# Turning attention weights by VectorE's 32x32 blocks and a DRAM scratch instead of by TensorE, in an attention and feed-forward kernel

## The chip, the cores and the metric

The kernel runs on one core of one Trainium2 chip. The metric is the device time of one execution in microseconds (us); below it is always the median of the fast runs of one kernel. Every ratio is between runs that took turns on the same chip; a difference between two experiments can go across sets of runs and chips, between which the median of the kernel before moved by 0.1%. A ratio is the mean time of one kernel's fast runs over the mean of the other's of the same rounds, so it is not quite the ratio of the medians that are quoted.

Engines: PE is TensorE's products, PEld its weight loads, DVE VectorE, ACT ScalarE, POOL GpSimd, SP SyncE, which here only issues DMAs.

## The reference, cut to what matters

```python
# q, k, v: 8 batches x 8 heads x 576 x 64, f32
scores = matmul(q, k.T) / 8
thresh = max(scores, axis=-1) - tau
attn   = exp(where(scores >= thresh, scores, -1e9) - max)   # then divided by its sum
x      = matmul(attn, v)            # (B, H, S, D) -> (B, S, 512)
xn     = (x - mean(x)) / sqrt(var(x) + 1e-6) * g_ln
out    = x + maximum(xn @ w_ch1, 0) @ w_ch2                 # 512 -> 2048 -> 512
```

All products are f32. The scores come out with queries on the partitions, and the product with v contracts over keys, so the normalised weights have to be turned in between. How they are turned is the change.

## The kernel before

A **unit** is two heads of one batch: 4 points of 128 queries for both heads, and a **rest point** (the last 64 queries of both heads together). There are 32 units, 4 per batch. A unit has 18 score products; the trace counts two records for an f32 product, so 36 records. The feed-forward part (FFN) works on groups of 512 tokens; group b is spread over the attention points of batch b + 1. A group has 128 products of 512 columns.

```python
def weights_of(u, j):                 # one point
    ...                               # TensorE: scores into sc (PSUM, two buffers)
    tensor_reduce(out=neg, in_=sc, op=max, negate=True)      # VectorE
    thr = -neg + low                                         # GpSimd
    activation(e, sc, Exp, bias=neg)                         # ScalarE
    scalar_tensor_tensor(e, sc >= thr, * e, accum_out=den)   # VectorE ("masking")
    reciprocal(den)                                          # VectorE
    e = e * den                                              # GpSimd

def turn_weights(u, j, es):
    for c in range(J):
        nc.tensor.transpose(tp[:, c], e[:, c * 128 : (c + 1) * 128], ident)
    nc.scalar.copy(em[...], tp)       # PSUM -> SBUF
    ...                               # the last 64 keys: two more transposes, two copies

def values_of(u, j):                  # after points 1, 3 and the rest point
    for c in range(J + 1):
        for h in range(2):
            nc.tensor.matmul(pv[...], lhsT=v, rhs=em)
    nc.vector.tensor_copy(x_of(g)[...], pv)
```

The program is written as one loop over points, with about two FFN steps (4 to 8 products) behind each. A scheduler then orders the instructions of each engine by its own model of their times. An engine runs its instructions in that order.

Of the kernel before, what the change touches and what calls it, by code (L numbers as in the profile page):

```python
# [8 lines left out]
F32 = mybir.dt.float32  # L9
# [9 lines left out]
def kernel(  # L19
# [44 lines left out]
    att = ctx.enter_context(tc.tile_pool(name="att", bufs=2))  # L64
    small = ctx.enter_context(tc.tile_pool(name="small", bufs=4))
    xpool = ctx.enter_context(tc.tile_pool(name="xpool", bufs=3))
    ps_sc = ctx.enter_context(tc.tile_pool(name="ps_sc", bufs=2, space=bass.MemoryType.PSUM))
# [15 lines left out]
    q_diag = [consts.tile([128, 128], F32, name=f"q_diag{i}") for i in range(2)]  # L83
    v_rest = [consts.tile([128, 2, D], F32, name=f"v_rest{i}") for i in range(3)]

# [3 lines left out]
    def load(u):  # L89


        b, hp = units[u]
        tiles = []
        for name, src in (("q", q), ("k", k)):
            t = ins.tile([128, NB, 32], F32, tag=name, name=f"{name}_in")
            for h in range(2):
                for e in range(2):
                    g = 2 * h + e
                    nc.sync.dma_start(
                        out=t[32 * g : 32 * g + 32],  # L100
                        in_=src[b, 2 * hp + h, :, 32 * e : 32 * e + 32].rearrange(
                            "(n r) c -> r n c", r=32
                        ),
                    )
            tiles.append(t)
        vt = ins.tile([128, J, 2, D], F32, tag="v", bufs=3, name="v_in")
        vr = v_rest[u % 3]
        for h in range(2):
            nc.sync.dma_start(
                out=vt[:, :, h, :],  # L110
                in_=v[b, 2 * hp + h, : J * 128, :].rearrange("(c p) d -> p c d", p=128),
            )
            nc.sync.dma_start(out=vr[64 * h : 64 * h + 64, h, :], in_=v[b, 2 * hp + h, J * 128 :, :])
        loaded[u] = (*tiles, vt, vr)
# [25 lines left out]
    )  # L140
    load(1)
    nc.gpsimd.dma_start(out=g_sb, in_=g_ln.rearrange("(c p) -> p c", p=128))
# [6 lines left out]
    def weight_steps(pool, which):  # L149
# [21 lines left out]
        for dst, src, gi in chunks:  # L171
            if src.dtype != I64:
# [4 lines left out]
                continue  # L177
            raw = pool.tile([128, WC], I64, tag="sq", name="raw")
            nc.gpsimd.dma_start(out=raw, in_=src)
            words = raw.bitcast(U32).rearrange("p (n two) -> p n two", two=2)  # L180
            lo, hi = words[:, :, 0], words[:, :, 1]
            a = pool.tile([128, WC], U32, tag="o", name="w_bits")
            r = pool.tile([128, WC], I32, tag="rb", bufs=1, name="w_low")
            m = pool.tile([128, WC], F32, tag="ot", name="w_kept")
            nc.scalar.activation(r, lo, func=AF.Copy, scale=2.0**-29)
# [17 lines left out]
            yield  # L203

    def turn(u):

        q_in, k_in = loaded[u][:2]
        qT = att.tile([128, J * 128], F32, tag="qT", name="qT")
        kT = att.tile([128, S], F32, tag="kT", name="kT")
        qd = q_diag[u % 2]  # L210
        nc.gpsimd.tensor_scalar(
            out=q_in, in0=q_in, scalar1=scl_sb, scalar2=1.0, op0=ALU.mult, op1=ALU.mult
        )
        nc.vector.transpose(kT, k_in.rearrange("p n c -> p (n c)"))  # L214
        nc.vector.transpose(qT, q_in[:, : J * 4].rearrange("p n c -> p (n c)"))
        for h in range(2):
            r = slice(64 * h, 64 * h + 64)
            nc.vector.transpose(qd[r, r], q_in[r, J * 4 :].rearrange("p n c -> p (n c)"))
        turned[u] = (qT, kT, qd)

    def weights_of(u, j):
# [20 lines left out]
        thr = small.tile([128, 2], F32, tag="thr", name="thr")  # L242
        es = []
        for i, sc in enumerate(scs):
            nc.vector.tensor_reduce(  # L245
                out=neg[:, i : i + 1], in_=sc[:, :, :HALF], axis=AXL.XY, op=ALU.max, negate=True
            )
            nc.gpsimd.tensor_scalar(  # L248
                out=thr[:, i : i + 1], in0=neg[:, i : i + 1], scalar1=-1.0, scalar2=low_sb,
                op0=ALU.mult, op1=ALU.add,  # L250
            )
            e = att.tile([128, S], F32, tag="e", bufs=4, name="e")
            nc.scalar.activation(  # L253
                e.rearrange("p (c n) -> p c n", c=2), sc[:, :, :HALF],
                func=AF.Exp, bias=neg[:, i : i + 1],
            )
            es.append(e)
        for i, (sc, e) in enumerate(zip(scs, es)):
            e2 = e.rearrange("p (c n) -> p c n", c=2)
# [12 lines left out]
    def turn_weights(u, j, es):  # L272


        if j in (0, 2, 4):
            n = 256 if j < J else 64
            em = att.tile([128, J, 2, 256], F32, tag="em", name="em")
            er = att.tile([128, 256], F32, tag="er", name="er")
            rounds[u] = (em, er, n)
        em, er, n = rounds[u]  # L280
        tr = ps_at.tile([128, 2, 128], F32, tag="at", name="tr")
        for h in range(2):
            e = es[h] if j < J else es[0]
            if j < J or h == 0:
# [3 lines left out]
                if j < J:  # L288
                    o = (j % 2) * 128
                    nc.scalar.copy(em[:, :, h, o : o + 128], tp)  # L290
                else:
                    nc.scalar.copy(
                        em[:, :, :, :64], tp.rearrange("p c (h t) -> p c h t", h=2)
                    )
# [4 lines left out]
        for h in range(2):  # L299
# [4 lines left out]
            else:  # L304
                nc.scalar.copy(er[r, :64], tr[r, h, r])  # L305

    groups = {}

# [4 lines left out]

    def values_of(u, j):

        b, hp = units[u]
        vt, vr = loaded[u][2:]
        em, er, n = rounds.pop(u)
        pv = ps_at.tile([128, 256], F32, tag="at", name="pv")
        for c in range(J + 1):  # L320
            for h in range(2):
                nc.tensor.matmul(  # L322
                    pv[64 * h : 64 * h + 64, :n],
                    lhsT=vt[:, c, h, :] if c < J else vr[:, h, :],
                    rhs=em[:, c, h, :n] if c < J else er[:, :n],
                    start=(c == 0), stop=(c == J),
                )
        t0 = b * S + (0, 0, 0, 256, 512)[j]
        at = 0
        while at < n:  # L330
            g, o = divmod(t0 + at, TOK)
            m = min(n - at, TOK - o)
            nc.vector.tensor_copy(x_of(g)[:, hp, o : o + m], pv[:, at : at + m])  # L333
            at += m
# [3 lines left out]
    def ffn_steps(g, x):  # L338

        sa = ffn.tile([128, 2, TOK], F32, tag="sq", name="sa")  # L340
        sm = ffn.tile([128, TOK], F32, tag="sm", bufs=1, name="sm")
        nc.gpsimd.tensor_tensor(out=sa, in0=x[:, 0:2], in1=x[:, 2:4], op=ALU.add)
        nc.gpsimd.tensor_tensor(out=sm, in0=sa[:, 0], in1=sa[:, 1], op=ALU.add)
        yield
        mean = ps_ff.tile([128, TOK], F32, tag="ff", name="mean")
        nc.tensor.matmul(mean, lhsT=avg_sb, rhs=sm, start=True, stop=True)
        xc = ffn.tile([128, NK, TOK], F32, tag="xc", bufs=1, name="xc")
# [4 lines left out]
        for i in range(2):  # L352
            sq = ffn.tile([128, 2, TOK], F32, tag="sq", name="sq")
            nc.scalar.activation(sq, xc[:, 2 * i : 2 * i + 2], func=AF.Square)
# [7 lines left out]
        def first(d):  # L362
            p1 = ps_ff.tile([128, TOK], F32, tag="ff", name="p1")
            for c in range(NK):
# [3 lines left out]
                )  # L368
            h = ffn.tile([128, TOK], F32, tag="h", bufs=ND + 1, name="h")
            nc.scalar.activation(h, p1, func=AF.Relu)  # L370
# [3 lines left out]
        for d in range(ND):  # L374
# [13 lines left out]
            if d == 11:  # L388
                rp = ps_ff.tile([128, TOK // 128, 128], F32, tag="ff", name="rp")
                for i in range(TOK // 128):  # L390
                    nc.tensor.transpose(
                        rp[:, i], rstd[:, i : i + 1].to_broadcast([128, 128]), ident
                    )
                rb = ffn.tile([128, TOK], F32, tag="rb", bufs=1, name="rb")
                nc.scalar.copy(rb, rp.rearrange("p i t -> p (i t)"))
                yield
        for m in range(NK):
            p2 = ps_ff.tile([128, TOK], F32, tag="ff", name="p2")
            for d in range(ND):
# [4 lines left out]
                if d % 4 == 3 and d < ND - 1:  # L404
                    yield
            o = ffn.tile([128, TOK], F32, tag="o", name="o")
            nc.vector.tensor_mul(o, p2, rb)  # L407
            nc.gpsimd.tensor_tensor(out=o, in0=o, in1=x[:, m], op=ALU.add)  # L408
            ot = ffn.tile([128, TOK // 32, 32], F32, tag="ot", name="ot")
            nc.vector.transpose(ot.rearrange("p n c -> p (n c)"), o)  # L410
            for i in range(4):
# [4 lines left out]
                    ),  # L416
                    in_=ot[32 * i : 32 * i + 32],
                )
# [35 lines left out]
    turn(0)  # L454
    held = None

    def finish(hu, hj, hes):
        turn_weights(hu, hj, hes)
        if hj in (1, 3, 4):
            values_of(hu, hj)  # L460
        if hj == J and units[hu][1] == HP - 1:
            after_batch(units[hu][0])

    for u in range(len(units)):
        for j in range(PTS):
            es = weights_of(u, j)
            if held is not None:
                finish(*held)
            held = (u, j, es)
            if j == 1 and u + 2 < len(units):  # L470
                load(u + 2)
            if j == 2 and u + 1 < len(units):
                turn(u + 1)
            for p in pumps:
                p.point()
    finish(*held)
    for p in pumps:
# [34 lines left out]
```

## Time and profile before

| part of the kernel before | us |
|---|---|
| batch 0, attention and conversion of W1 | 158 |
| batch 1, with conversion of W2 | 206 |
| batches 2 to 6 | 192 each |
| batch 7 | 188 |
| tail: the last two FFN groups | 243 |
| whole | 1757.66 (1757.14 to 1758.93, 3 runs) |

Parts are read from the starts of the FFN groups' means in the profiled run. Two rows of the page show how evenly TensorE is fed: the span in 40 slices, with its busy share in tenths and the granted TensorE clock in tenths.

```profile
PE   4889899999999999999999999999999999999998
...
PEclk9789899999999999999999999999999999999999
```

The group of the score products, with their busy time and the idle time of TensorE just before them with what ended it:

```profile
L236 PE MATMUL sc<-kT,qT 64*128 64x288 f32 x1024 | 196.0, 455 | 26.7 <-DVE kT L214 15.2 <-DVE e L260 11.5
```

Over 1024 records TensorE waited 11.5 us for VectorE's masking.

### The profile page before, as it was taken

What the parts mean: (1) busy time and instruction counts of PE and PEld (TensorE: products, weight loads), DVE (VectorE), ACT (ScalarE), POOL (GpSimd) and SP (SyncE); (2) the same over time, 40 slices, a digit from 0 to 9 for tenths busy, and PEclk for the clock granted to TensorE, in tenths of its full rate; (3) what the DMA queues carried; (4) which work ended last, traced back from release to release, by engine and by line L of the source; (5) the groups of instructions that cost most, each with busy time, mean ns of one, the idle gap of its engine ahead of it and who ended that gap; (6) DMA issues with size and microseconds to landing.
All of it is one profiled execution on the core that took longest, in us unless ns stands there. A gap on an engine that the chain in (4) does not pass through costs nothing.

```text
span 1757.6 us, 19852 instructions
## 1 busy us (share of the span) xinstructions
PE 1665.7 (95%) x6974; PEld 849.2 (48%) x6974; DVE 678.8 (39%) x1561; ACT 627.0 (36%) x1220; POOL 527.2 (30%) x789
## 2 busy tenths in 40 slices
PE   4889899999999999999999999999999999999998
PEld 2545445545554555545544555455454555444443
DVE  5766544433444334343334434444344434200000
ACT  6775863234323342234323432234223422220110
POOL 6765842232224122232233212322233122300100
PEclk9789899999999999999999999999999999999999
DMA  7423410111111111111111111101111000001001
GB/s 155 108 69 66 133 41 16 33 27 21 21 33 33 21 21 17 31 19 21 26 28 33 21 21 33 33 11 21 27 23 27 7 1 12 13 0 18 6 5 20
DMA packets 271380, 55.83 MB, mean 32 GB/s; under 512 B 267184, under 2 KB 267184, under 8 KB 271280
## 3 DMA queue, kind: packets, MB, share of 16 engines
q1 hardware_dynamic: 266640, 37.78, 12.3%
q0 software_dynamic: 4640, 16.78, 3.3%
q8 instruction: 55, 0.90, 0.2%
q14 instruction: 45, 0.37, 0.1%
HBM read 45.09 MB, written 9.44 MB: 31 GB/s over the span
## 4 chain that ended last, share of the span: by engine, by line
PE 82%; DVE 5%; ACT 5%; POOL 3%; DMA 2%; issue 2%; SPq 0%; ACTq 0%; POOLq 0%; DVEq 0%
PE p L400 27%; PE p L365 26%; PE pv L322 11%; PE sc L236 11%; PE tp L287 6%; DVE neg L245 2%; ACT e L253 2%; DMA raw<-in_moe_w_ch_dram 2%; ACT em L290 1%; DVE xc L348 1%; PE tr L296 1%; ACT er L303 1%; PE tr L298 1%; DVE e L260 1%; POOL o L408 1%
## 5 line engine op out<-in xcount | busy, mean ns | idle before, releaser
L365 PE MATMUL p<-xc,w 128*128 128x512 f32 x1152 | 541.5, 608 | 10.3 <-DVE xc L348 9.8
L400 PE MATMUL p<-h,w 128*128 128x512 f32 x1152 | 525.2, 597 | 0.0
L245 DVE TENSOR_REDUCE neg<-sc 128x1 f32<-128x576 f32 x288 | 207.3, 750 | 477.3 <-PE sc L236 476.9
L253 ACT ACTIVATE e<-sc,neg 128x576 f32<-128x576 f32 x288 | 212.5, 745 | 373.5 <-DVE neg L245 368.0
L365 PEld LDWEIGHTS p<-xc,w 128*128 128x128 f32 x1152 | 207.3, 193 | 222.1 <-issue 208.2
L400 PEld LDWEIGHTS p<-h,w 128*128 128x128 f32 x1152 | 206.6, 190 | 218.5 <-issue 218.0
L265 POOL TENSOR_SCALAR e<-e,den 128x576 f32<-128x576 f32 x288 | 215.9, 752 | 250.1 <-DVE den L264 216.9
L248 POOL TENSOR_SCALAR thr<-neg,low_sb 128x1 f32<-128x1 f32 x288 | 78.8, 274 | 625.6 <-DVE neg L245 599.0
L260 DVE SCALAR_TENSOR_TENSOR e<-sc,thr,e 128x576 f32<-128x576 f32 x288 | 232.1, 812 | 54.9 <-ACT e L253 36.4
L236 PE MATMUL sc<-kT,qT 64*128 64x288 f32 x1024 | 196.0, 455 | 26.7 <-DVE kT L214 15.2
L370 ACT ACTIVATE h<-p 128x512 f32<-128x512 f32 x144 | 85.9, 596 | 364.7 <-PE p L365 364.3
L290 ACT COPY em<-tp 128x512 f32<-128x512 f32 x256 | 149.2, 583 | 177.4 <-PE tp L287 174.9
L287 PEld LDWEIGHTS tp<-ident,e 128*128 128x128 f32 x1152 | 134.8, 145 | 145.4 <-ACT em L290 75.1
L287 PE MATMUL tp<-ident,e 128*128 128x128 f32 x1152 | 188.9, 288 | 16.8 <-ACT em L290 14.1
L322 PE MATMUL pv<-em,v_in 128*64 128x256 f32 (+1 forms) x1536 | 176.1, 350 | 7.9 <-ACT er L303 6.3
L236 PEld LDWEIGHTS sc<-kT,qT 64*128 64x128 f32 x1024 | 106.1, 198 | 136.5 <-issue 80.7
L322 PEld LDWEIGHTS pv<-em,v_in 128*64 128x64 f32 x1536 | 98.9, 142 | 114.9 <-issue 30.8
L408 POOL TENSOR_TENSOR o<-o,x 128x512 f32<-128x512 f32 x36 | 45.5, 1265 | 274.7 <-DVE o L407 274.7
L407 DVE TENSOR_TENSOR o<-p,rb 128x512 f32<-128x512 f32 x36 | 24.9, 692 | 200.7 <-PE p L400 200.7
L333 DVE COPY x<-pv 128x256 f32<-128x256 f32 (+3 forms) x120 | 35.4, 311 | 168.6 <-PE pv L322 168.6
L322 PE MATMUL pv<-er,v_rest 128*64 128x256 f32 (+1 forms) x384 | 62.9, 342 | 15.2 <-ACT er L305 15.2
L303 ACT COPY er<-tr 64x128 f32<-64x128 f32 x256 | 65.7, 257 | 2.3 <-PE tr L298 0.7
(61 smaller groups left out, 857.8 us busy)
## 6 DMA issues: line engine op xcount, KB each, us to landing
raw<-in_moe_w_ch_dram POOLq DMA_DIRECT2D x32, 512.0 KB, 4.2
q_in<-in_q_dram SPq DMA_DIRECT2D x128, 72.0 KB, 2.5
k_in<-in_k_dram SPq DMA_DIRECT2D x128, 72.0 KB, 2.3
out_dram<-ot SPq DMA_DIRECT2D x144, 64.0 KB, 1.9
v_in<-in_v_dram SPq DMA_DIRECT2D x64, 128.0 KB, 2.4
v_rest<-in_v_dram SPq DMA_DIRECT2D x64, 16.0 KB, 2.1
tau_sb<-in_tau_dram SPq DMA_DIRECT2D x1, 0.5 KB, 2.6
g_sb<-in_moe_g_ln_dram POOLq DMA_DIRECT2D x1, 2.0 KB, 3.5
```

What stands on the lines that cost most here:

```text
L236: nc.tensor.matmul(sc[:, c, :HALF], lhsT=lhsT, rhs=kT[rows, c * HALF : (c + 1) * HALF], start=True, stop=True,)
L245: nc.vector.tensor_reduce(out=neg[:, i : i + 1], in_=sc[:, :, :HALF], axis=AXL.XY, op=ALU.max, negate=True)
L253: nc.scalar.activation(e.rearrange("p (c n) -> p c n", c=2), sc[:, :, :HALF], func=AF.Exp, bias=neg[:, i : i + 1],)
L260: nc.vector.scalar_tensor_tensor(out=e2, in0=sc[:, :, :HALF], scalar=thr[:, i : i + 1], in1=e2, op0=ALU.is_ge, op1=ALU.mult, accum_out=den ...
L265: nc.gpsimd.tensor_scalar(out=e, in0=e, scalar1=den[:, i : i + 1], scalar2=1.0, op0=ALU.mult, op1=ALU.mult)
L287: nc.tensor.transpose(tp[:, c], e[:, c * 128 : (c + 1) * 128], ident)
L290: nc.scalar.copy(em[:, :, h, o : o + 128], tp)
L303: nc.scalar.copy(er[r, o : o + 128], tr[r, h])
L322: nc.tensor.matmul(pv[64 * h : 64 * h + 64, :n], lhsT=vt[:, c, h, :] if c < J else vr[:, h, :], rhs=em[:, c, h, :n] if c < J else er[:, :n ...
L365: nc.tensor.matmul(p1, lhsT=w1_sb[c][:, d * 128 : (d + 1) * 128], rhs=xc[:, c, :], start=(c == 0), stop=(c == NK - 1),)
L370: nc.scalar.activation(h, p1, func=AF.Relu)
L400: nc.tensor.matmul(p2, lhsT=w2_sb[d][:, m * 128 : (m + 1) * 128], rhs=hs[d], start=(d == 0), stop=(d == ND - 1),)
```

## The change

TensorE is the bound, and 1.25 us of each point are transposes on it. The change takes them off it from batch 1 on: VectorE turns each weight tile within 32x32 blocks, SyncE writes the blocks to a DRAM scratch so that a row of the scratch is one key, and reads it back with keys on the partitions. The value products come some points later, and their sums are copied out of PSUM by ScalarE instead of VectorE.

```diff
+    def turn_blocks(u, j, es):
+        ...
+        for h, et in enumerate(rounds[u]):
+            nc.vector.transpose(et[:, :, j % 2], es[:, h].rearrange("p (n c) -> p n c", c=32))
+            if j % 2 == 1:
+                for a in range(4):
+                    nc.sync.dma_start(out=scr[h, :, :, a]..., in_=et[32 * a : 32 * a + 32]...)
+    def fetch(j, scr):
+        ...
+        for h in range(2):
+            nc.sync.dma_start(out=em[:, h, :, :n], in_=rows[h, : J * 128]...)
+            nc.sync.dma_start(out=er[64 * h : 64 * h + 64, :n], in_=rows[h, J * 128 :])
...
-            nc.vector.tensor_copy(x_of(g)[:, hp, o : o + m], pv[:, at : at + m])
+            (nc.scalar.copy if by_blocks(u) else nc.vector.tensor_copy)(
+                x_of(g)[:, hp, o : o + m], pv[:, at : at + m]
+            )
...
+        if by_blocks(u):              # every batch but the first
+            scr = turn_blocks(u, j, es)
+            if ends:                  # points 1, 3 and the rest point
+                later(1, lambda: later(2, values, u, j, fetch(j, scr)))
```

The cuts (`...`) leave out tile shapes, the smaller buffers of q, k and the FFN that make room, and the order of the columns of q. The weights' two exponential buffers of a point (e) are one tile now, with two in all.

## The prediction

> **What bounds the kernel now.** I read the page first (busy shares), then busy time by stretch, then the chain of work that ended last in one stretch, then groups by shape, then VectorE's timeline in a stretch without feed-forward work. A line with x8 counts records; one f32 product is two records, so x8 is four products.
>
> Busy time by stretch (us; columns PE, PEld, DVE, ACT, POOL busy with counts, granted clock, DMA share, GB/s):
>
> ```profile
> core 0: us, PE busy (x) PEld busy (x) DVE busy (x) ACT busy (x) POOL busy (x), PEclk, DMA share, GB/s
> 120.00:158.00 38.00, 34.23 (x212) 21.45 (x212) 24.67 (x62) 20.10 (x44) 18.64 (x29) 0.96 0.16 28
> 158.00:365.00 207.00, 194.51 (x826) 98.14 (x828) 94.89 (x208) 100.10 (x186) 95.26 (x125) 0.96 0.25 58
> 942.00:1134.00 192.00, 187.92 (x842) 96.73 (x841) 78.20 (x187) 66.77 (x135) 51.41 (x85) 0.99 0.14 25
> 1518.00:1758.00 240.00, 227.90 (x538) 101.39 (x538) 14.57 (x21) 25.87 (x41) 20.89 (x14) 0.97 0.06 10
> ```
>
> The mean of a feed-forward (FFN) group comes at 158, 364, 556, 750, ... us. So the kernel is: batch 0, attention alone with the weight conversion, 158 us; batch 1, 207 us; batches 2 to 7, 192 us each; a tail of 240 us with only FFN. In a 192 us batch TensorE is busy 98% and VectorE 41%: TensorE is the bound. The chain in one such stretch (start, length, what) shows which TensorE work is on the path:
>
> ```profile
> 708.05 1.17 PE sc L236 x8
> 709.22 0.59 PE tp L287 x4
> 709.80 0.11 PE tr L296
> 709.91 0.11 PE tr L298
> 710.02 1.72 PE p L400 x4
> 711.74 0.44 PE tp L287 x4
> 712.18 5.15 PE p L400 x12
> ```
>
> One attention point (one 128-query block of two heads) costs 1.17 us of scores, 0.59 + 0.11 + 0.11 + 0.44 = 1.25 us of transposes, and FFN products at 5.15 / 12 x 2 = 0.86 us each fill the rest. The transposes stand on the path with nothing beside them.
>
> **What the Trainium skill says.** (1) "TensorE: Matmul & The Clock Gate", Part 2, step LDWEIGHTS: "The MATMULs themselves stay in program order"; only weight loads are pulled ahead. The trace agrees: the order of products in the timeline is that of the built program (8 score records, 4, 1, 1 transposes, 4, 4, 12). So a product that waits holds all behind it, ready or not. (2) "VectorE: DVE Perf Modes", The three transpose paths: VectorE transposes only within 32x32 blocks, so the rest has to be done by addresses, here through DRAM. In this trace a 128x576 block transpose takes 0.77 us. (3) "DMA: Bandwidth & Descriptors", Two DMAs through the same engine are not ordered: a read of what a DMA wrote has to wait at the issuing engine for the write's semaphore. So SyncE's queue stands still for it; this trace has no such pair. (4) The first page, HAM oscillation: gaps above about 3.4 us lower the clock. The trace agrees in kind: 0.78 granted in 40 to 80 us, where TensorE waits often, 0.99 in full batches.
>
> **The change part by part.**
> Removed from TensorE: per unit (two heads, 5 points; 28 units in batches 1 to 7) 36 + 10 transposes at 0.11 us (0.44 / 4) plus about 0.15 us after each score block (0.59 - 0.44): 46 x 0.11 + 5 x 0.15 = 5.8 us, x 28 = 162 us. Removed from ScalarE: the copies out of PSUM, about 7.5 us per unit.
>
> Added to VectorE: nine block transposes per unit, 9 x 0.77 = 6.9 us; the x copies (35.4 us / 32 = 1.1) go to ScalarE. VectorE's attention work per unit is then, from these rows,
>
> ```profile
> L260 DVE SCALAR_TENSOR_TENSOR e<-sc,thr,e 128x576 f32<-128x576 f32 x288 | 232.1, 812 | 54.9 <-ACT e L253 36.4 <-POOL thr L248 9.4 <-ACT em L290 0.6
> ...
> L245 DVE TENSOR_REDUCE neg<-sc 128x1 f32<-128x576 f32 x288 | 207.3, 750 | 477.3 <-PE sc L236 476.9
> ...
> L264 DVE RECIPROCAL den<-den 128x1 f32<-128x1 f32 x288 | 45.0, 161 | 5.9
> ...
> L214 DVE STREAM_TRANSPOSE kT<-k_in 128x576 f32<-128x576 f32 x32 | 24.6, 769 | 0.0
> ```
>
> (232.1 + 23.9 for its accumulator reads + 207.3 + 45.0) / 32 = 15.9, plus 2.0 for turning q and k, plus 6.9 = 24.8 us, or 99 per batch of 192.
>
> Added to SyncE: 20 scratch writes and 12 reads per unit beside 12 loads and 4 stores; an issue takes 0.5 us in its timeline, so about 25 us per unit. Added to the DMA engines: 11,520 write packets and 3,456 read packets per unit; the hardware queue now needs 12.3% x 1757.6 x 16 / 266,640 = 13 ns per packet. With larger packets I estimate 20 to 26 us per unit over 16 engines. All three fit under a batch's 192 / 4 = 48 us per unit. If that were all, the time would fall by 162 us.
>
> **Where I chose otherwise: the order.** The built program of the changed kernel doesn't just lack the transposes. Before, in batches 1 to 7 never more than 7 FFN products follow each other without attention between them, and each point has about 6.4 of them. Changed, the scheduler has put each group's 128 FFN products first (runs of up to 34) and then a long row of attention alone. In batch 5, counted from 0: all 128 FFN products stand beside only 26 of 72 score products and 50 of 120 value products; then come 46 score and 70 value products with nothing else. Batches 1 to 7 have 44, 44, 48, 40, 46, 46, 34 score products in such rows, 302 of 504. Since TensorE doesn't reorder, it will wait there for VectorE and ScalarE, and FFN work that could fill the waits has been spent.
>
> What a unit costs when alone: batch 0's end is such a stretch, with no FFN and no conversion on VectorE:
>
> ```profile
> 147.26 0.82 DVE L260 SCALAR_TENSOR_TENSOR e<-sc,thr,e 128x576 f32<-128x576 f32 x1 [0.59 <-ACT e L253]
> ...
> 148.00 0.75 DVE L245 TENSOR_REDUCE neg<-sc 128x1 f32<-128x576 f32 x1
> ...
> 149.93 0.76 DVE L245 TENSOR_REDUCE neg<-sc 128x1 f32<-128x576 f32 x1 [0.31 <-PE sc L236]
> ...
> 152.47 0.82 DVE L260 SCALAR_TENSOR_TENSOR e<-sc,thr,e 128x576 f32<-128x576 f32 x1 [0.58 <-ACT e L253]
> ```
>
> Ten masking operations start between 128.3 and 154.8 us, 2.65 us apart; a unit has nine, so 24 us per unit, with VectorE busy 19.05 of 27 us and the gaps ended by ScalarE and by the scores. The changed unit: 24 + 6.9 - 1.1 = 29.8 us. Walking the changed order by hand for one unit gives the same: 24.8 busy plus about 5 of waits (scores only after both maskings of the point before, 1.1 us twice; exponentials for a buffer that the block transposes free, 0.85 twice; 0.7 once).
>
> **The sum.** (a) Batch 0, unchanged on TensorE: 158. (b) FFN rows: 7 x 113 (112 per group from the tail plus the mean) + (504 - 302) x 0.293 = 59 for scores + 320 value products at about 0.2 = 63: 913. (c) Waits in them: before each group TensorE now has nothing beside copy, two sums on GpSimd (2.35 + 1.26), mean and centring (2.27), some 7 us, plus 3 for scores packed too close: 7 x 10 = 70. (d) Attention alone: the last 3 products of each row overlap (c), so (302 - 21) / 18 = 15.6 units x 29.8 = 465. (e) Batch 1's weight conversion, as before (207 - 192): 14. (f) The last unit's way through DRAM: 12. (g) Tail: 240. Together 158 + 913 + 70 + 465 + 14 + 12 + 240 = 1872; I say 1870.
>
> **The rivals.**
> A: the intended gain. TensorE stays the bound and all else hides: 1758 - 162 = about 1600. For it: 98% busy and the 0.44 us of pure transposes on the chain. Against it: the fixed order; even with VectorE never idle, (d) is 15.6 x 24.8 = 387 and the sum without (c) is 1724.
> B: the rows of attention alone are bound by VectorE without idle time and the waits in FFN rows are half as long: 1872 - 78 - 35 = 1759, the same time. Against it: VectorE was only 70% busy in the stretch above.
> C: SyncE's queue or the DMA engines set the pace of these rows. Loads stand in SyncE's order between the scratch write and its read, and the load of v waits there for value products of the unit before; about 25 us of issue plus waits for landing is close to 29.8. If it takes 34 us: 15.6 x 4.2 = 66 more, 1938. The clock speaks the same way: at 0.8 granted each block of scores takes 0.3 us longer, some 3 us per unit with the products behind them.
>
> **Range and chances.** A unit alone between 26 and 34 us moves (d) by -59 to +66; (c) may be 30 to 110. Together 1790 to 1960. Faster by over 2% (below 1722) needs the rows to run at VectorE's bare sum with almost no other wait: 0.03. Within 2% (to 1793): 0.12. Slower: 0.85.
>
> **What would show it.** Steps right: busy time by stretch shows each batch of some 205 to 215 us split into about 135 us with TensorE above 90% and 70 to 80 us with TensorE near 40% and VectorE above 80%; transposes by TensorE fall to an eighth; idle time of score products ended by VectorE's masking grows from 12 us to over 200. Wrong if FFN products are spread through the batch, if TensorE is above 90% busy throughout (A), if VectorE is over 95% busy in the rows (B), or if value products wait mainly for reads of the scratch and SyncE issues without pause (C).

## The result, and the profile after

The changed kernel is correct and takes 2083.41 us (2078.88 to 2084.05, 4 runs) against 1757.4 (4 runs): ratio 1.185, interval 1.183 to 1.187, slower. The mean granted clock is 0.853 against 0.974.

The same two rows of the page, now of the changed kernel:

```profile
PE   5898996699867996699868996699867997689898
...
PEclk9779997699858996699968996689967998689999
```

Seven dips, one for each batch from 1 to 7, in busy share and in clock. Busy time by stretch shows what the dips are. The columns are as in the prediction: us; PE, PEld, DVE, ACT, POOL busy with counts; granted clock, DMA share, GB/s. The stretches are batch 1, batch 4 (each split at the last FFN product of its run) and the tail.

```profile
156.00:318.00 162.00, 148.23 (x442) 66.31 (x443) 79.00 (x159) 66.86 (x105) 78.57 (x96) 0.97 0.47 120
318.00:410.00 92.00, 58.20 (x249) 33.44 (x249) 52.46 (x114) 16.43 (x31) 26.85 (x47) 0.65 0.77 167
887.00:1026.00 139.00, 134.97 (x398) 60.27 (x397) 37.31 (x79) 25.54 (x40) 21.61 (x32) 0.97 0.31 73
1026.00:1106.00 80.00, 49.57 (x222) 28.26 (x221) 49.72 (x109) 14.65 (x25) 25.56 (x44) 0.67 0.77 172
1823.00:2082.00 259.00, 237.79 (x580) 106.14 (x580) 16.16 (x20) 26.51 (x43) 20.84 (x14) 0.94 0.08 17
```

A batch first has its FFN, dense, at full clock (139 us, TensorE 97% busy), then a row of attention alone (80 us, TensorE 62% busy at a clock of 0.67). The prediction had TensorE near 40% and VectorE above 80% in such a row. VectorE is busy 62% of it: nothing is at its limit there. The score products, again with the idle time before them:

```profile
L251 PE MATMUL sc<-kT,qT 64*128 64x288 f32 x1024 | 338.0, 564 | 202.1 <-DVE e L274 189.3 <-DVE kT L222 12.5
```

11.5 us of waiting for the masking have become 189.3, and the products themselves take 338 instead of 196 us, since most of the late ones run at the low clock. DMA is not what TensorE waits for: in the rows alone VectorE waits less than 0.1 us a unit for the scratch, and TensorE 0.3, although the hardware queue's packets grew from 12.3% to 40.3% of the 16 engines' time. In the whole kernel the value products waited for the scratch twice (us in total, times, longest):

```profile
PE pv L380 <- DMA em<-scr: 5.2, 2, 3.3
```

Set against the terms of the prediction, the trace has:

| term | predicted us | measured us |
|---|---|---|
| (a) batch 0 | 158 | 156 |
| (b) + (c) + (e) FFN rows, waits in them, conversion | 913 + 70 + 14 = 997 | 1031 |
| (d) + (f) attention alone, last way through DRAM | 465 + 12 = 477 | 636 |
| (g) tail | 240 | 259 |
| sum | 1872 | 2082 |

The measured rows of attention alone run from the last FFN product of a batch to the next mean and hold 604 score records, the 302 products that the prediction had counted in the built order: 16.8 units of 36 records. Three quarters of the miss is term (d), and most of that is the pace of a unit.

### The profile page after: what moved, and what is told of

The parts are those of the page before. It is cut to its first block, busy times and chain, and to the rows that moved or that the text cites. A ratio compares the mean times of both kernels' runs of the same rounds, so it can differ in the third digit from the quotient of the medians.

```text
span 2082.3 us, 18243 instructions
## 1 busy us (share of the span) xinstructions
PE 1749.1 (84%) x5686; PEld 845.3 (41%) x5686; DVE 812.0 (39%) x1733; ACT 468.9 (23%) x796; POOL 532.0 (26%) x790
## 3 DMA queue, kind: packets, MB, share of 16 engines
q1 hardware_dynamic: 700304, 186.48, 40.3%
## 4 chain that ended last, share of the span: by engine, by line
PE 68%; DVE 8%; DMA 7%; issue 5%; SPq 5%; POOL 4%; ACT 3%; DVEq 0%; POOLq 0%; ACTq 0%
PE p L424 24%; PE p L459 22%; PE sc L251 12%; PE pv L380 8%; DVE e L274 3%; DMA raw<-in_moe_w_ch_dram 2%; ACT e L267 2%; DMA em<-scr 2%; SPq L345 2%; DVE et L342 2%; DVE xc L407 1%; DVE neg L260 1%; POOL sa L401 1%; DMA scr<-et 1%; SPq L329 1%
## 5 line engine op out<-in xcount | busy, mean ns | idle before, releaser
L251 PE MATMUL sc<-kT,qT 64*128 64x288 f32 x1024 | 338.0, 564 | 202.1 <-DVE e L274 189.3
L251 PEld LDWEIGHTS sc<-kT,qT 64*128 64x128 f32 x1024 | 184.4, 243 | 338.3 <-issue 287.2
L380 PE MATMUL pv<-em,v_in 128*64 128x256 f32 (+1 forms) x1536 | 239.3, 421 | 5.7 <-DMA em<-scr 5.2
L380 PEld LDWEIGHTS pv<-em,v_in 128*64 128x64 f32 x1536 | 130.6, 172 | 140.0 <-issue 112.0
L468 POOL TENSOR_TENSOR o_both<-o_both,x 128x512 f32<-128x512 f32 x36 | 45.6, 1266 | 481.8 <-DVE o_both L467 481.5
L342 DVE STREAM_TRANSPOSE et<-e 128x576 f32<-128x576 f32 x224 | 159.7, 748 | 2.2 <-POOL e L279 2.1
L391 ACT COPY x<-pv 128x256 f32<-128x256 f32 (+3 forms) x108 | 28.2, 285 | 490.3 <-PE pv L380 489.7
L251 PE MATMUL sc<-kT,q_diag 128*128 128x288 f32 x128 | 54.7, 564 | 27.9 <-DVE e L274 27.9
L380 PEld LDWEIGHTS pv<-er,v_rest 128*64 128x64 f32 x384 | 45.6, 161 | 16.7 <-issue 10.1
L251 PEld LDWEIGHTS sc<-kT,q_diag 128*128 128x128 f32 x128 | 29.1, 252 | 54.5 <-issue 46.3
```

The source lines that it names most:

```text
L251: nc.tensor.matmul(sc[:, c, :HALF], lhsT=lhsT, rhs=kT[rows, c * HALF : (c + 1) * HALF], start=True, stop=True,)
L342: nc.vector.transpose(et[:, :, j % 2], es[:, h].rearrange("p (n c) -> p n c", c=32))
L380: nc.tensor.matmul(pv[64 * h : 64 * h + 64, :n], lhsT=vt[:, c, h, :] if c < J else vr[:, h, :], rhs=em[:, h, c, :n] if c < J else er[:, :n ...
L468: nc.gpsimd.tensor_tensor(out=o, in0=o, in1=x[:, m], op=ALU.add)
```

## The experiments

Two questions: is the order the cause of the slowdown, as the prediction said, and why was a unit alone so slow? The pace is given in two ways. The expectations use the length of the rows over their score records, times 36. They put it at 36.4 us for the changed kernel and at 29.8 for e5; counted anew (604 records in 636 us, 584 in 494) it is 37.9 and 30.4. The table at the end uses the distance from one rest point's scores to the next one's inside a row (36.7), which leaves the ends of the rows out. "ScalarE waits for sums" is ScalarE's idle time before copies of value sums in those rows, per unit of 36 records (the expectations say 18.0 for the changed kernel and 5.3 for e5; counted anew 18.7 and 5.4).

Order is fixed in the experiments by pinning an instruction behind all those that were written before it on its engine.

### First set: is it the order?

The theories are named by letter: O, the order in which TensorE meets its work; S, the new way through SyncE's queue and the scratch; V, VectorE's new work.

**e1_pinned.** Score, value and FFN products of batches 1 to 7 stay on TensorE in the order in which the program was written, with FFN steps between the points.

```diff
+                if by_blocks(u):
+                    pin(mm)           # mm: a score product, likewise a value product
...
-                nc.tensor.matmul(p1, ...)
+                pin(nc.tensor.matmul(p1, ...))     # likewise p2
```

> The changed kernel with every TensorE product from batch 1 on pinned behind the product written before it, so that each attention point is followed by its 6 or so FFN products as in the kernel before; nothing else changes. Theory O (the order of the products on TensorE is what costs): a batch is TensorE's own work without transposes, 192 - 28 of transposes and the waits behind them = about 165 us, plus a few us at the group boundary, so 158 + 14 + 7 x 167 + 245 = about 1590, range 1560 to 1650. Rival S (the path through the scratch, SyncE's queue above all, cannot supply a unit in time in any order): value products wait for reads of the scratch, batches stay at 190 us or more, 1750 or more.

Measured: correct, 1661.38 us (1659.54 to 1666.14), ratio 0.945. The same instructions in another order are 422 us faster than the changed kernel and faster than the kernel before. O holds. Some 70 us of the best case are missing; one batch shows where:

```profile
886.00:1060.00 174.00, 165.56 (x654) 79.50 (x654) 98.44 (x211) 43.03 (x74) 50.77 (x85) 0.96 0.67 149
```

174 us with 165.56 busy, against 192 before. Five of the eight means before the tail's last stand behind a wait of 4.9 us for GpSimd's sum, and seven run at half clock (2.1 us for the two records). In the batch shown the next scores then wait another 2.0 us for VectorE's masking, which stands behind the centring. Batch 1 (212 us) and the tail (249 us) gain nothing either.

**e2_write_on_act.** The scratch writes on ScalarE's queue, order left to the scheduler.

```diff
-                    nc.sync.dma_start(out=scr[h, :, :, a]..., in_=et...)
+                    nc.scalar.dma_start(out=scr[h, :, :, a]..., in_=et...)
```

> The changed kernel with the scratch writes issued by ScalarE's queue instead of SyncE's; reads, loads and stores stay. In the built program the FFN products are then spread over the batch again (runs of up to 21 to 26, but nearly every attention block has some beside it). Theory O: 1600 to 1750, rows of attention alone short or gone. Rival S in the form that SyncE's issue time as such costs on the chip: about the same gain. Rival V (VectorE's added transposes set the pace of attention): no gain, above 2000.

Measured: correct, 1913.45 us (1910.07 to 1917.32), ratio 1.088, neither range. The scheduler spreads the FFN more (the rows alone shrink from about 90 to about 30 us a batch), but the value products now wait for the scratch reads, as this line of the waits says (us in total, times, longest):

```profile
PE pv L380 <- DMA em<-scr: 155.5, 47, 10.3
```

In the changed kernel they hardly waited for reads. The eight writes of a round take 11.0 us from first to last issue on ScalarE, against 5.9 on SyncE in the changed kernel (medians). The run shows that the queue's place steers the scheduler; as a test of O alone it is unclean.

**e3_transposes_back.** Transposes by TensorE in every batch, all other edits of the change kept.

```diff
     def by_blocks(u):
-        return units[u][0] > 0
+        return False
```

> The changed kernel with the block path switched off in all batches: TensorE turns the weights again, every other edit of the change stays (one tile for both heads' weights, single buffers for q and k, later loads, shared buffers for weight conversion and outputs). Theory O: these edits cost nothing, 1757 within 1%. Rival B (the buffers given up for the new tiles cost): 1800 or more.

Measured: correct, 1749.39 us, ratio 0.995. The other edits cost nothing.

**e4_before_front.** The kernel before, with nothing changed but that each FFN group from the second on is given out over 8 points instead of 20.

```diff
-        pumps.append(Pump(ffn_steps(b, groups.pop(b)), FFN_STEPS, points))
+        pumps.append(Pump(ffn_steps(b, groups.pop(b)), FFN_STEPS, points if b == 0 else 8))
```

> The kernel before, with TensorE transposes and all else as it was, except that each FFN group from batch 2 on is handed out over 8 points of the batch instead of 20, so that rows of attention alone follow, as in the changed kernel. Theory O: 11 or 12 points alone per batch at 24 us or more per unit, where a spread batch hides them: 10 to 25 us more in each of 6 batches, 1820 to 1910, and the granted clock in those rows falls to 0.8 or less. Rival S or V: the order costs little by itself, 1757 within 1.5%.

Measured: correct, 1880.36 us, ratio 1.068. A batch of this kernel takes 211 us instead of 192:

```profile
1002.00:1213.00 211.00, 202.47 (x838) 103.79 (x838) 76.86 (x184) 67.24 (x134) 50.66 (x83) 0.98 0.13 22
```

"FFN first" alone costs the old kernel 123 us, with its transposes still on TensorE. So the pattern is a loss in itself, and the change made the scheduler choose it.

### Second set: what sets the pace of a unit alone?

**e5_front_pinned.** The order of e1 pinned, but FFN first on purpose: the base of the next runs.

```diff
-        pumps.append(Pump(..., FFN_STEPS, points))
+        pumps.append(Pump(..., FFN_STEPS, 12 if b == 0 else 8))     # on e1_pinned
```

> The changed kernel with its instruction order written down instead of left to the scheduler: score, value and FFN products pinned in program order as in e1_pinned, but each FFN group given out over the first 8 (first group: 12) of the 20 attention points, so that the other 12 run alone, which is what the scheduler made by itself. It is the base for the next three, which change one thing each in the same TensorE order. If order is the cause, it comes back to the changed kernel's time: 2040 to 2110 us, with a granted clock near 0.65 and about 36.5 us a unit in the rows alone. If something else of the scheduler's order made the loss (loads, stores, DVE order), it stays under 1950.

Measured: correct, 1913.37 us (1910.18 to 1916.02), ratio 1.088. The first branch of the expectation missed by over 120 us, and its other branch holds ("stays under 1950"): a pattern that looks like the changed kernel's is 170 us faster. One batch, dense part and row alone:

```profile
819.00:955.00 136.00, 133.02 (x398) 60.62 (x398) 40.96 (x86) 24.32 (x38) 23.04 (x36) 0.96 0.37 85
955.00:1022.50 67.50, 42.76 (x201) 22.62 (x200) 47.65 (x103) 15.74 (x26) 24.29 (x42) 0.70 0.80 178
```

TensorE is 63% busy at a clock of 0.70 in the row, about as in the changed kernel, but a unit takes 30.4 us by the row's length (31.3 from rest point to rest point). That is close to the predicted 29.8, in part by luck: between rest points VectorE is busy 22.5 us and idle 8.8, where the prediction had 24.8 and about 5. Of the 170 us, 142 lie in the rows alone (636 against 494), 23 in the dense parts.

**e6_front_warm.** Three extra products after the scores of each point alone, to keep the clock up.

```diff
+        if by_blocks(u) and all(p.done >= p.steps for p in pumps):
+            warm = ps_ff.tile([128, TOK], F32, tag="ff", name="warm")
+            for _ in range(3):
+                pin(nc.tensor.matmul(warm, lhsT=avg_sb, rhs=w1_sb[0][:, :TOK], start=True, stop=True))
```

> e5_front_pinned with three FFN-sized products into a spare PSUM tile after the scores of each point that runs alone (84 points, no reader, right result). It adds 2.6 us of TensorE work at full clock to a point of 7.3 us. Theory C (the row alone is long because TensorE falls to half clock in it): the clock in rows alone rises above 0.85, a group of 8 score records goes from 3.0 to about 1.2 us, and the time falls by 50 to 110 us to 1970 to 2035. Theory Q (SyncE's issue queue sets the pace): TensorE's clock does not matter, no fall of more than 20 us. If TensorE's added work itself were on the path, it would rise by up to 220 us.

Measured: correct, 1882.63 us, ratio 1.071; 31 us less than e5. The row alone has its clock back:

```profile
944.00:1021.00 77.00, 71.83 (x335) 34.28 (x335) 58.78 (x130) 18.96 (x31) 28.78 (x51) 0.98 0.86 188
```

0.98 instead of 0.70, and a unit falls by 1.9 us only (31.3 to 29.4). The 31 us lie between the two forecasts (50 to 110, and at most 20). They are a net figure: the extra products take TensorE's time too (it is busy 27.6 of the 29.4 us), and VectorE still waits 2.4 us a unit for scores. So the low clock costs at least 1.9 us a unit in e5; how much more is not shown.

**e7_front_act.** e5 with the scratch writes on ScalarE's queue.

> e5_front_pinned with the scratch writes (20 of about 46 issues a unit) on ScalarE's queue, in the same TensorE order. Theory Q: SyncE loses 13 to 15 us of issue time a unit, and the rows alone come down by 50 to 110 us: 1970 to 2035. Theory C: within 25 us of e5, still at a clock near 0.65. If ScalarE, now blocked while it waits for transposed blocks, takes over as the pace, it rises.

Measured: correct, 1969.7 us, ratio 1.120: 56 us slower. In the rows alone ScalarE then stands some 14.6 us a unit in two rounds of issues (7.37 and 7.21 us in the unit from 1010 to 1046 us), and exponentials stand behind them. The Trainium skill ("Perfetto Trace Analysis", DMA Optimizations, item 3) says that balancing DMAs over the engines that can issue them may help if descriptor generation is the bottleneck. SyncE issued for 25 of 30 us a unit in e5, yet relieving it lost time: the queue that took over was one with work of its own, and nothing here shows SyncE's issuing as the bottleneck.

**e8_front_warm_act.** Both edits.

> Both edits of e6 and e7. If clock and queue lie so close that each alone hides the other (C and Q both), only this one falls: each alone under 40 us, both together 90 us or more below e5. If C alone holds it equals e6; if Q alone, e7.

Measured: correct, 2009.81 us, ratio 1.142, slower than either. No run separates why the extra products, which helped e5, cost 40 us here.

**e9_x_on_dve.** The changed kernel, with the copies of the value sums back on VectorE.

```diff
-            (nc.scalar.copy if by_blocks(u) else nc.vector.tensor_copy)(
+            nc.vector.tensor_copy(
```

> The changed kernel with one part undone: the copies of the value sums from PSUM (x) go back from ScalarE to VectorE. The TensorE order stays as good as the same. Seen so far: a unit alone takes 36.4 us in the changed kernel and 29.8 with the order pinned (e5), at the same clock (0.67 against 0.70), and ScalarE waits 18.0 us a unit for value products in front of such a copy, against 5.3 in e5. Theory R (ScalarE, in order, stands at a copy while the next exponentials could run): the unit falls by 3 to 5 us, the time by 50 to 90 us to 1990 to 2035. Theory E (the exponentials wait for one of only two e buffers, whatever ScalarE does): 2070 to 2100, since VectorE gets 1 us more a unit.

Measured: correct, 2109.32 us, ratio 1.198. Slower, both ranges missed. In the rows VectorE now waits 4.2 us a unit for value sums, where it waited for none, and ScalarE waits for VectorE instead. The wait moved along with the copies.

**e10_four_e.** The changed kernel with four e tiles; two pairs of W1 tiles share memory, so the result is wrong.

```diff
-    w1_sb = [consts.tile(...) for i in range(NK)]
+    w1_sb = [consts.tile(...) for i in range(2)] * 2
...
-        es = att.tile([128, 2, S], F32, tag="e", name="e")
+        es = att.tile([128, 2, S], F32, tag="e", bufs=4, name="e")
```

> The changed kernel with four e buffers instead of two; room for them by letting two pairs of W1 tiles share memory, so the result is wrong on purpose, with the same work. The FFN clumps in the built order stay. Theory E: the exponentials' waits for block turns (6.3 us a unit) go, the unit falls by 3 to 5 us, the time to 1990 to 2035. Theory R: 2060 to 2100, as ScalarE still stands at its copies.

Measured: wrong, 2129.13 us, ratio 1.210, neither range. The built order changed as well: in the rows TensorE now waits 4.2 us a unit for the turned k, which it did not do in the changed kernel. So the run does not price the buffers; ScalarE's wait for value sums (24.0 us a unit) is still there in it.

**e11_lagged**, a version and not a test: e1 with each group's mean two points behind its first sum, and the last products of the group before in the gap.

```diff
+            if self.late:
+                n = min(self.at, 2) + max(0, -(-(self.steps - 2) * (self.at - 2) // self.over))
```

> A try for the best version, not a test of a cause: e1_pinned (1661) with each FFN group's mean two points behind its first sum and its products from the third point on, while the last products of the group before fill these two points. In e1 the stretch around each mean costs about 9 us a batch (4.9 waiting for the sum, 2.1 at half clock, 2 for xc). If that stretch is filled: 1600 to 1630. If it moves to another wait: 1650 or more.

Measured: correct, 1605.66 us (1598.99 to 1606.91), ratio 0.912. One batch:

```profile
866.00:1025.00 159.00, 159.00 (x655) 76.65 (x654) 98.93 (x210) 42.74 (x74) 50.82 (x85) 1.00 0.74 164
```

TensorE is busy all 159 us at full clock. This is the gain that the change was meant to have.

**e12_front_lump.** e5 with the value products of a unit's second round one point later, in one lump with the rest point's.

```diff
-                later(1, lambda: later(2, values, u, j, fetch(j, scr)))
+                later(1, lambda: later(3 if j == 3 else 2, values, u, j, fetch(j, scr)))
```

> e5_front_pinned with one thing changed: the value products of a unit's second round (256 tokens) are given one point later, so that they stand in one lump of 20 with those of the rest round, before the next scores, as in the changed kernel's rows (there: 4 score products, 1 value product, 4 score products, 19 value products). Nothing is added. The runs before (e9, e10) killed both single causes: moving the copies to VectorE only made VectorE stand there (4.4 us a unit), four e buffers did not help. Theory L (the lump: the copy of its sums stands in the order of an in-order engine ahead of the next exponentials or turns, and so the next scores come late): the unit goes from 29.8 to 33 to 37 us, the time from 1913 to 1965 to 2030. If the lump is harmless and the pace comes from VectorE's or ScalarE's order alone: 1900 to 1935.

Measured: correct, 1956.84 us, ratio 1.113: 43 us slower, more than a harmless lump would make and less than theory L said; a unit takes 0.6 us more by rest points (31.9), 2.0 by the row's length.

**e13_copies_late.** The changed kernel with ScalarE's exponentials and copies pinned so that both copies of the lump stand behind the rest point's exponential.

```diff
+        if by_blocks(u):
+            later(2 if j == 3 else 1, copies, u, j, pv, n)     # the copies, on their own
...
+            if by_blocks(u):
+                pin(ex)               # exponential; likewise each copy
```

> The changed kernel with ScalarE's exponentials and copies pinned in an order in which the two copies of the lump (second round and rest) stand behind the rest point's exponential (four exponentials, two copies, five exponentials becomes five, two, four). The TensorE order in the rows alone stays the same: 4 score products, 1 value product, 4, 19, 10, 10. If ScalarE's order is the cause: a unit alone falls from 36.4 to 31.5 to 34, the time from 2083 to 2000 to 2045. If the exponential was not late for the copies: within 15 us of 2083.

Measured: correct, 2011.0 us, ratio 1.144, as expected; a unit falls to 34.6 us (35.1 by the row's length, a little above the expected 34). Pinning ScalarE's order is worth 72 us. By stretch, 33 of them are in the rows alone and 34 in the dense parts, whose order moved a little too.

Most of the wait only moved on. ScalarE waits 230 us less for sums in the whole kernel (lines below, at e16) and 196 us more for VectorE's block transposes, which free the e buffers. The waits for these, of the changed kernel, of e13 and of e5:

```profile
ACT e L267 <- DVE et L342: 161.5, 23, 26.5
```

```profile
ACT e L269 <- DVE et L346: 357.1, 43, 30.3
```

```profile
ACT e L271 <- DVE et L346: 158.6, 31, 13.2
```

**e14_act_pinned.** The changed kernel with exponentials and copies pinned as written, which puts most copies ahead, but takes most lumps of value products apart on TensorE.

> The changed kernel with the exponentials and copies of ScalarE pinned in traced order and nothing else. The built TensorE order keeps the FFN clumps, but in the rows alone value products mostly stand in tens between the scores, as in e5; one lump of 19 a batch is left. If attention's own order in the rows alone makes the missing 6.6 us a unit: a unit at 30 to 32, the time 1970 to 2010. If the e5 pace needed the whole pinned order: above 2040.

Measured: correct, 2082.39 us, ratio 1.185: no gain, the second branch of the expectation. With the copies ahead (ScalarE waits 22.0 us a unit for sums), taking value products apart brought nothing in this run.

**e15_copies_first** and **e16_copies_behind.** e5 with the lump behind the rest point's scores, as in the changed kernel, and the copies of a point's sums once before and once behind the exponentials of the point. Both also pin ScalarE's exponentials and copies. The two differ in one line's place.

```diff
-        run_due(sums)                 # e15: value products and copies, then exponentials
         ...                           # the exponentials of the point
+        run_due(sums)                 # e16
```

> e5_front_pinned (29.8 us a unit alone) rebuilt toward the changed kernel: the lump of 20 value products stands behind the rest point's scores, and ScalarE's copies of every sum stand ahead of the exponentials of the same point. If the copies' place makes the missing time: 34.5 to 38 us a unit, ScalarE waiting 15 us or more a unit for sums, 1990 to 2055 us. If the pinned kernel keeps its pace all the same: 31 to 33 us a unit, 1930 to 1970.

> The same kernel and TensorE order as e15, with the copies behind the exponentials of the point. Theory: 3 to 6 us a unit less than e15, 50 to 100 us in all: 1920 to 1970. If the lump's place on TensorE is what costs, e15 and e16 agree within 20 us.

Measured: e15 correct, 2048.88 us, ratio 1.164; e16 correct, 2008.46 us, ratio 1.142. The copies' place is worth 40 us (4.1 us a unit), a little under the expected 50; e16 itself is higher than expected, so the lump's place on TensorE, or the pinned ScalarE, costs as well. In the whole kernel ScalarE waits for sums, of e15 and of e16:

```profile
ACT x L400 <- PE pv L387: 557.9, 71, 16.6
```

```profile
ACT x L400 <- PE pv L387: 181.7, 48, 10.3
```

In the changed kernel and in e13 the same line has:

```profile
ACT x L391 <- PE pv L380: 489.7, 76, 22.7
```

```profile
ACT x L402 <- PE pv L384: 260.2, 44, 25.8
```

**e17_late_and_four_e.** e13's edit and four e tiles (wrong result).

> e13 (copies behind the rest point's exponential) with e10's four e buffers (two pairs of W1 tiles share memory; wrong result on purpose). If copies and buffers hide each other: a unit alone at 30 to 32.5 us from rest point to rest point, 1920 to 1975 us, well below both e13 (2011) and e10 (2129). If buffers don't matter even with the copies out of the way: 2000 to 2030.

Measured: wrong, 2106.42 us, ratio 1.197; a clear miss. The four tiles changed the order that the scheduler built, and the copies stand ahead of exponentials again (ScalarE waits 21.8 us a unit for sums), so this was no test of both together. But its trace shows the copies' part with the buffers out of the way. Timelines of one point on VectorE, TensorE and ScalarE (start, length, idle before it and what ended that):

```profile
1063.05 1.65 DVE L262 TENSOR_REDUCE neg<-sc 128x1 f32<-128x576 f32 x2 [1.25 <-PE sc L253]
...
1073.35 0.82 DVE L278 SCALAR_TENSOR_TENSOR e<-sc,thr,e 128x576 f32<-128x576 f32 x1 [5.58 <-ACT e L269]
```

```profile
1067.78 3.25 PE L384 MATMUL pv<-em,v_in 128*64 128x256 f32 x13 [1.49 <-DMA em<-scr]
...
1070.82 1.44 PE L384 MATMUL pv<-er,v_rest 128*64 128x256 f32 x3
1074.32 0.96 PE L253 MATMUL sc<-kT,qT 64*128 64x288 f32 x3 [2.06 <-DVE e L278]
```

```profile
1072.30 0.37 ACT L402 COPY x<-pv 128x256 f32<-128x256 f32 x1 [11.73 <-PE pv L384]
1072.57 1.38 ACT L269 ACTIVATE e<-sc,neg 128x576 f32<-128x576 f32 x2
```

The maxima are there at 1064.7, and the exponentials need only them and a buffer; VectorE's last block transpose before them ended at 1065.4. They start at 1072.57, because the copy in front of them on ScalarE waits for value products that themselves wait for the scratch and run to 1072.26. VectorE idles 5.58 us for the exponentials, and the next scores wait for VectorE. The Trainium skill ("TensorE: Matmul & The Clock Gate", Part 1, Architectural detail) says "ACT/DVE are strict FIFO"; the trace agrees, with 11.73 us of ScalarE idle while the exponentials behind the copy had their data for 7 us.

### All of the second set together

| run | us | unit alone, us | ScalarE waits for sums, us a unit |
|---|---|---|---|
| e6 (e5, clock kept up) | 1883 | 29.4 | 6.4 |
| e5 (FFN first, pinned) | 1913 | 31.3 | 5.4 |
| e12 (e5, lump before the rest point) | 1957 | 31.9 | 7.0 |
| e13 (changed, copies late) | 2011 | 34.6 | 8.0 |
| e16 (e5, lump behind, copies behind) | 2008 | 34.7 | 8.8 |
| changed kernel | 2083 | 36.7 | 18.7 |
| e15 (e5, lump behind, copies first) | 2049 | 38.8 | 18.8 |
| e10 (changed, four e) | 2129 | 39.4 | 24.0 |
| e17 (copies late and four e) | 2106 | 40.3 | 21.8 |
| e14 (changed, ScalarE as written) | 2082 | 40.4 | 22.0 |

Where ScalarE waits under 9 us for sums a unit takes at most 34.7; where it waits 18 or more, at least 36.7.

## Why the prediction was right or wrong, point by point

**The bound before, and the transposes on its path: right.** e11 gets 152 us below the kernel before with the same parts; the removed work was put at 162.

**FFN first, then attention alone: right, and it is the cause of the slowdown.** Pinning the order turns 1.185 into 0.945 (e1), and the pattern alone costs the kernel before 6.8% (e4). The direction was predicted from the built order, and it held. The signs named for it held in part: TensorE's transposes fell to an eighth (144 of 1152), and the scores' idle time ended by masking is 217 us with the rest points' 27.9, but batches take 219 to 254 us instead of 205 to 215.

**(b), (c), (e), the FFN rows: 34 us too low.** No experiment split these terms. The stalls at each mean are there as (c) had them: in the changed kernel's trace TensorE waits 4.1 and 4.2 us for GpSimd's sum before the means at 887 and 1106 us, and 2.45 us for the centred tile behind the first of them.

**(d), attention alone: the failed step, 159 us too low with (f).** Its mechanism was right and two factors were off.
First, the number of units: 15.6 predicted, 16.8 measured. The rows hold the 302 products that were counted; the prediction had taken off 21 of them, on the argument that the last three of each row overlap (c). At 29.8 us each that is 35 us.
Second, the pace: 29.8 predicted, 37.9 measured, 8.1 us over 16.8 units, 136 us. (The two make 171; the 159 has the 12 us of (f) set against them.) The prediction added two figures, batch 0's 24 us and the block turns, and then came to the same number by walking the changed order by hand, with "24.8 busy plus about 5 of waits". VectorE's busy time was indeed no more than that (22.7 us between rest points); it was idle for 14.0 more: 8.8 for scores, 4.3 for exponentials. So the waits of the walk are what failed. It gave the exponentials 0.85 us twice to wait for a buffer, and no copy to stand behind. In the changed kernel's rows they start 3.05 us behind their maxima on average, in e5 0.69. At the rest point (6.5 us late, median) a copy stands ahead: the change had put the copies of the value sums on ScalarE, and the scheduler placed two or three of them ahead of the rest point's exponential, behind a lump of value products. At points 1 and 2, counted from 0 (4.7 and 5.1 us late), the buffer ends the wait: VectorE's block transposes, which free it, come late.

What the runs settle of those 5.4 us (36.7 against e5's 31.3, by rest points): the copies' place makes 2.1 (the changed kernel against e13) to 4.1 (e15 against e16). The place of the value products on TensorE makes 0.6 (e12) to 3.4 (e16 against e5). The changed kernel and e13 differ in the dense parts too, and e5 and e16 in ScalarE's pinning, so these don't add up term by term. A third part stands untested: VectorE's order was pinned in no run, and the two runs with more buffers (e10, e17) got other orders. The traces speak for it. From the first scores of the rest point to its exponential it takes 9.1 us in the changed kernel, 7.1 in e13 and 3.8 in e5 (means); in e13 and e5 the wait ends 0.1 us behind the first block transpose of point 3. The steps of 2.0 and 3.3 are nearly those of the unit (36.7, 34.6, 31.3). That this is their cause is not shown, and e16, at 4.6 with a unit of 34.7, says that it is not all. Nor is the 34 us settled that e13 gained in the dense parts.

**(g), the tail: 19 us too low.** Three of them are the tail before, which is 243 by the same reading; and more value products stand in it now (40 records instead of 20). It was not tested.

**Rival A (1600) was the gain that the parts allow**, and e11 has it at 1606; the prediction was right that the built order would not give it. **Rival B** falls: VectorE is 62% busy in the row. **Rival C**, the queue and the clock: relieving SyncE's queue brought nothing (e7; the run stands on e5 and puts the issues on ScalarE, so a part isn't ruled out), and the clock, as low as 0.65, is worth 1.9 us a unit or more in e5 (e6, a net figure). It was named for the right region of time; as the main cause neither run bears it out.

## What to carry to other kernels

When a change takes work off the bounding engine, compare the built order on every engine before counting the gain: a scheduler that works by a model may answer by putting all ready work first and leaving rows in which the bound waits, and pinning the written order can be worth more than the change. When you cost such a row, walk the order of every engine in it, also the idle ones: a short copy that waits for a product, placed ahead of an exponential, holds up all that follows, and so does a transpose that comes late and keeps a buffer. And an engine moved off the bound's path isn't free to take "a few copies": what matters is not how long they take but what they wait for.

## What the Trainium skill lacked or had wrong

- "TensorE: Matmul & The Clock Gate", HAM oscillation, counts what a lowered clock costs the products. It lacks that raising the clock by extra products can bring little where TensorE waits anyway: from 0.70 to 0.98 in the rows alone, 31 of 1913 us net (e6).
- "Perfetto Trace Analysis", DMA Optimizations, lacks the price of spreading DMAs to an engine with other work: some 14.6 us a unit in rounds of issues on ScalarE, 56 us more in all, although SyncE had been issuing for 25 of 30 us (e7).
- "VectorE: DVE Perf Modes", The three transpose paths, gives one bf16 size. In these traces a 128x576 f32 block transpose takes 0.73 to 0.78 us on VectorE, and with the scratch a 144 KB write landed in 2.9 us and a 512 KB read in 5.0 us (e1, medians).
- No page has the cost of an instruction's place in an idle engine's order: the same copies, before or behind the exponentials, make 40 us of 2049 (e15, e16).
